# Exchanging odd v products and odd q products between two stages, and running w3's last columns in four column groups

## The chip, the cores and the metric

The kernel runs on one core of a Trainium2 chip. The core has a matrix engine (TensorE, PE in the profile, with its weight loads shown as PEld), a vector engine (VectorE, DVE), a scalar engine (ScalarE, ACT), GpSimd (POOL), and SyncE (SP), whose queue issues this kernel's DMA transfers in order. Every engine works through its own list of instructions and waits on semaphores for the others. Matmuls read SBUF and write PSUM, which has eight banks; one bank holds 128 x 512 f32 values.

The metric is the device time of one execution in microseconds (us). Lower is better.

## What is computed

A gated block over 2048 rows of 512 features, in bf16. `xn` is the layer norm of `x`; `s` is a sliding dilated attention of 32 heads of 16 features, each position looking at 8 positions, 2 apart; `g` is a token-shifting MLP.

```python
def _A_ref(x, wqkv, wo):                      # x is xn here
    qkv = transpose((x @ wqkv).reshape(B, S, 3, 32, 16), 2, 0, 3, 1, 4)
    q, k, v = qkv
    idx = pos[:, None] - 2 * arange(8)[None, :]       # positions before 0 are masked
    logits = einsum("bhsd,bhswd->bhsw", q, k[:, :, idx]) * 16 ** -0.5
    o = einsum("bhsw,bhswd->bhsd", softmax(logits), v[:, :, idx])
    return o.transpose(...).reshape(B, S, 512) @ wo

def _B_ref(x, w1, w2, w3, w4):                # w3 is 512 x 1376, w4 is 1376 x 512
    h = gelu(layernorm(x) @ w1)
    # four quarters of h's columns, shifted by +1, -1, +2, -2 rows
    x1 = x + concatenate([g0, g1, g2, g3], -1) @ w2
    return x1 + gelu(layernorm(x1) @ w3) @ w4

xn = layernorm(x)
out = x + _A_ref(xn, wqkv, wo) * silu(_B_ref(xn, w1, w2, w3, w4))
```

## The kernel before

**Rows.** The attention looks back by steps of two, so even and odd rows never meet in it. The kernel keeps them apart: `p` = 0 for the even rows, 1 for the odd ones, 1024 rows each. A chunk `c` is 512 rows of one parity: chunks 0 and 1 are even, 2 and 3 odd. `xnT[p]` holds the normalized rows transposed, features on partitions.

**Order.** Every instruction is wrapped in `pin`, which keeps it in program order on its engine, so each engine's list is as the code is written, the SP queue's too. A wait at the head of a list holds up all that is behind it.

**PSUM.** In the first stage `pair()` gives two banks at a time out of three pairs in turn (banks 0 to 5), and `single()` banks 6 and 7. The matmuls for a pair wait until the pair three before it has been read.

**First stage, lines 501 to 622.** Rows are loaded, normalized and transposed. Then, chunk by chunk, come the products: `q_all(c)` is two pairs of eight matmuls, each pair copied to `qT` by ScalarE; `k_all(c, parts, both)` the same for k, where each pair is copied twice under two head masks (with `both=False` VectorE takes half of the copies); `v_pair(p, t)` is two 128-row tiles of v, one ScalarE copy into one of two staging buffers `vst`, and two stores to `v_d` in DRAM, 256 KB each; `w1(c, a)` is half of a chunk's first MLP layer with a gelu. `w1` reads `xn2T`, which `scaled(c)` makes on VectorE from `xnT` and row factors that go through DRAM (`rows2_write`, `rows2_read`). `w2(c)` adds the second layer to the rows and takes the statistics of the second norm; `columns(c)` applies that norm and issues four transposing DMAs into `x1nT`. `v_pad` stores zero rows around v. Then `w3(c)` for four chunks: 1376 columns are ten blocks of 128 and one of 96, each block four matmuls; gelus go to `h3a` and `h3b`. In this kernel the even rows' v is computed here and the odd rows' v is not; q and k are computed here for all rows. `w4_sb` is loaded at line 599, in the middle of this stage, after `k_all(2)`.

**Attention, lines 911 to 983.** There are 18 turns `n` (`NU`), 9 for each parity. A turn issues `scores(n)` (32 small matmuls in four row groups and an exp on ScalarE into `prob`; all scores share banks 0 to 3), the minimum with a mask for the turn before (`band`), and `values(n-2)`: 32 matmuls in four column groups for the output (L675), 16 more in four column groups for the softmax denominators (L685), and a copy to `oT`. Between them TensorE is given w4's products: `g_w4(t)` is a `Group` of 11 matmuls for a tile of 128 rows, and `w4_take(k)` issues up to `k` of them in order; `q` in line 914 is a turn's quota, taken in thirds. The last product of a group lets VectorE add the bank to the rows (L800), and then a tanh and a gate follow. With each turn comes one smaller group (`small_g`): in turns 0 to 7 `g_v(n)`, one tile of the odd rows' v (four matmuls, a ScalarE copy, and a store at the turn's end); later `g_fin`, the output product with wo, for even rows. While `w4_take` runs with `extra`, the small group is issued right when a w4 group ends, and if at most 5 of the turn's quota are then left, these are dropped and made up by the next turns. Groups use banks 6 and 7 in turn through the list `free`.

Denominators of a batch of turns end in turns 5, 9, 13 and 16 (`ends`), where `inverse` makes their reciprocals on VectorE (L697) and `write_rec` stores them; `read_rec` and `apply` use them one to three turns later.

**Tail, from line 985.** The last w4 products, and the output products of the odd rows with their stores.

**Buffers.** `b8` tiles (8 KB a partition) share 11 buffers and `b4` tiles (4 KB) 10; a tile's buffer is free again after its last use. `wqk_sb` is a `b8` tile with the weights of q and k.

Of the kernel before, what the change touches and what calls it, by code (L numbers as in the profile page):

```python
# [8 lines left out]
AF = mybir.ActivationFunctionType  # L9
# [11 lines left out]
def kernel(  # L21
# [19 lines left out]
    def pin(ins):  # L41

        return tc.keep_in_program_order(ins)
# [30 lines left out]
    big = ctx.enter_context(tc.tile_pool(name="big", bufs=11))  # L74
    kbp = ctx.enter_context(tc.tile_pool(name="kbp", bufs=2))
    wpl = ctx.enter_context(tc.tile_pool(name="wpl", bufs=2))
    sm4 = ctx.enter_context(tc.tile_pool(name="sm4", bufs=10))
    fin = ctx.enter_context(tc.tile_pool(name="fin", bufs=8))
    dram = ctx.enter_context(tc.tile_pool(name="dram", bufs=1, space=bass.MemoryType.DRAM))
    psp = ctx.enter_context(tc.tile_pool(name="psp", bufs=1, space=bass.MemoryType.PSUM))  # L80
# [1 line left out]
    def b8(shape, name):  # L82
        return big.tile(shape, BF16, name=name, tag="b8")

    def b4(shape, name):
        return sm4.tile(shape, BF16, name=name, tag="b4")
# [4 lines left out]
    def pair():  # L91
        cnt["d"] += 1
        b = 2 * ((cnt["d"] - 1) % 3)
        return PS[:, b : b + 2, :]
# [11 lines left out]
            out=xn[p][:, i : i + n, :], in_=xv[p, i * P : (i + n) * P, :].rearrange("(i q) d -> q i d", q=P)  # L106
        ))

    wqk_sb = b8([P, ND, 2 * D], "wqk_sb")
    wv_sb = b4([P, ND, D], "wv_sb")  # L110
    load_x(0, 0, 1)
    load_x(0, 1, 1)
# [2 lines left out]
    load_x(0, 3, 1)  # L115
    for h in range(2):
        pin(SP.dma_start(
            out=wqk_sb[:, :, h * D // 2 : (h + 1) * D // 2], in_=wqkv_v[:, :, h * D // 2 : (h + 1) * D // 2]
        ))
    pin(SP.dma_start(out=wqk_sb[:, :, D : 2 * D], in_=wqkv_v[:, :, D : 2 * D]))  # L120
    load_x(1, 0, 2)
    load_x(1, 2, 2)
    w1_sb = b4([P, ND, D], "w1_sb")
# [166 lines left out]
    def scaled(c):  # L290
        p, k = c // 2, c % 2
        t = xn2Ts[c]
        pin(DVE.tensor_tensor(  # L293
            out=t, in0=xnT[p][:, :, k * CH : (k + 1) * CH],
            in1=t[:, ND - 1, :].unsqueeze(1).to_broadcast([P, ND, CH]), op=ALU.mult,
        ))
# [27 lines left out]
    def q_half(pts, lo, hi, nts=range(ND)):  # L324
        for nt in nts:
            for dt in range(ND):
                pin(PE.matmul(  # L327
                    pts[nt // 2][:, nt % 2, lo:hi], lhsT=wqk_sb[:, dt, nt * P : (nt + 1) * P],
                    rhs=xnT[0][:, dt, lo:hi], start=(dt == 0), stop=(dt == ND - 1),
                ))  # L330

    def proj(c, a, w, rhs):
        pt = pair()
        for b in range(2):
            nt = 2 * a + b
            for dt in range(ND):
                pin(PE.matmul(  # L337
                    pt[:, b, :], lhsT=w[:, dt, nt * P : (nt + 1) * P], rhs=rhs[:, dt, :],
                    start=(dt == 0), stop=(dt == ND - 1),
                ))  # L340
        return pt

    def chunk(t, c):
        p, k = c // 2, c % 2
        return t[p][:, :, k * CH : (k + 1) * CH]

    def q_keep(c, a, pt):
        pin(ACT.activation(chunk(qT, c)[:, 2 * a : 2 * a + 2, :], pt, AF.Copy))

    def q_all(c):  # L350
        for a in range(2):
            q_keep(c, a, proj(c, a, wqk_sb[:, :, 0:D], chunk(xnT, c)))

    def k_pad(p):
        pin(POOL.memset(kM[p][:, :, 0:8, :], 0.0))
# [2 lines left out]
    def k_all(c, parts=(0, 1), both=True):  # L358

        p, k = c // 2, c % 2  # L360
        for a in parts:
            pt = proj(c, a, wqk_sb[:, :, D : 2 * D], chunk(xnT, c))
            for e in range(2):
                dst = kM[p][:, 2 * a : 2 * a + 2, 8 + k * CH : 8 + (k + 1) * CH, e]
                sc = em[:, e : e + 1]
                if both:
                    pin(ACT.activation(dst, pt, AF.Copy, scale=sc))  # L367
                else:
                    pin(ACT.activation(dst[:, 0], pt[:, 0], AF.Copy, scale=sc))
                    pin(DVE.tensor_scalar(out=dst[:, 1], in0=pt[:, 1], scalar1=sc, scalar2=None, op0=ALU.mult))  # L370
# [40 lines left out]
    def w1(c, a):  # L411
        p, k = c // 2, c % 2
        pt = proj(c, a, w1_sb, xn2Ts[c])
        pin(ACT.activation(  # L414
            hT[p][:, 2 * a : 2 * a + 2, 1 + k * CH : 1 + (k + 1) * CH], pt, AF.Gelu_apprx_tanh
        ))
# [51 lines left out]
    def h3_of(c, ft):  # L468
        return h3a[c][:, ft, :] if ft < NA else h3b[c][:, ft - NA, :]

    def w3(c):
        x1nT = x1nTs.pop(c)
        h3a[c] = b8([P, NA, CH], "h3a")
        h3b[c] = b4([P, NF - NA, CH], "h3b")
        for a in range((NF + 1) // 2):
            pt = pair()
            fts = [ft for ft in (2 * a, 2 * a + 1) if ft < NF]
            for ft in fts:
                fs = P if ft < NF - 1 else FL
                for dt in range(ND):  # L480
                    pin(PE.matmul(  # L481
                        pt[:fs, ft % 2, :], lhsT=w3_sb[:, dt, ft * P : ft * P + fs], rhs=x1nT[:, dt, :],
                        start=(dt == 0), stop=(dt == ND - 1),
                    ))
            if len(fts) == 2:
                t, o = (h3a[c], 2 * a) if 2 * a < NA else (h3b[c], 2 * a - NA)
                pin(ACT.activation(t[:, o : o + 2, :], pt, AF.Gelu_apprx_tanh))  # L487
            else:
                pin(ACT.activation(h3b[c][:FL, NF - 1 - NA, :], pt[:FL, 0, :], AF.Gelu_apprx_tanh))

    xo = {}

# [99 lines left out]
    w1(1, 0)  # L592
    w1(1, 1)
    scaled(2)
    q_all(2)
    k_all(2, (0,))
    scaled(3)
    k_all(2, (1,), both=False)
    pin(SP.dma_start(
        out=w4_sb[:, 0 : NF - 1, :],  # L600
        in_=B_w4[0 : (NF - 1) * P, :].rearrange("(ft q) n -> q ft n", q=P),
    ))
    pin(SP.dma_start(out=w4_sb[0:FL, NF - 1, :], in_=B_w4[(NF - 1) * P : F, :]))
    w1(2, 0)
    w1(2, 1)
    w1(3, 0)
    w2(0)
    w1(3, 1)
    columns(0)
    v_pad(1)  # L610
    q_all(3)
    k_all(3)
    w2(1)
    w2(2, "a0 a1 c- s0 s1")
    w3(0)
# [4 lines left out]
        load_xo(0, i)  # L620
    for c in range(1, NCH):
        w3(c)


    pin(ACT.preload_act_table_set("exp_and_others"))
# [126 lines left out]
            out=ov[p, i * P : (i + n) * P, :].rearrange("(i q) d -> q i d", q=P), in_=xo[p][:, i : i + n, :]  # L752
        ))

    tanhs, gates, vstores = [], [], []

    free = [6, 7]

# [54 lines left out]

        return Group(NF, one, done)

    def g_v(t):
        def one(pt, dt):
            pin(PE.matmul(  # L818
                pt, lhsT=xnT[1][:, dt, t * P : (t + 1) * P], rhs=wv_sb[:, dt, :],
                start=(dt == 0), stop=(dt == ND - 1),  # L820
            ))

        return Group(ND, one, lambda pt: v_keep(1, t, 1, pt, vstores))

    stores = []
    now = {"n": 0}
# [40 lines left out]

    finals = []
    w4s = [g_w4(t, 2 if t == 15 else int(t > 12)) for t in range(16)]
    small_g = {n: [g_v(n)] for n in range(8)}  # L870
    fin0 = [g_fin(0, i, SP if i % 2 else None, later=finals) for i in range(8)]
    fin1 = [g_fin(1, 0, later=finals)]
    for n, i in zip((8, 9, 10, 12, 13, 14, 15, 16), range(8)):
# [3 lines left out]
    def flush(q):  # L877
        while q:
            q.pop(0)()
# [31 lines left out]
    load_va(0)  # L911
    for n in range(NU):
        now["n"] = n
        q = W4 * (n + 1) // NU - kept_back.get(n, 0) - unit["given"]
        extra = small_g.get(n, [])

        early = n < 8
        if n == 0:
            unit["left"] = HEAD
            w4_take(HEAD)  # L920
            unit["given"] = 0
        unit["left"] = q

        for j in range(2):
            if n == NU - 1:
                read_rec(3, 2 * j, 2)
            elif n - 1 - j in ends:
                read_rec(ends[n - 1 - j], 2 * j, 2)
        if n == 15:
            values(13)  # L930
        scores(n)
        if 1 <= n < 16:
            band(n - 1)
        if n >= 2 and n != 15:
            values(n - 2 if n < 16 else n - 1)
        if n + 1 < NU:
            load_va(n + 1)
        if n == 4:
            load_wo()
        if n != 16:  # L940
            flush(finals)
        if n in ends:
            recs[ends[n]] = inverse()
            write_rec(ends[n])
        if n == 17:
            free += [2, 3]
            pin(ACT.preload_act_table_set("silu_and_others"))
        w4_take(5 if n == 15 else q // 3)
        late = list(gates)
        gates.clear()  # L950
        flush(tanhs)
        if n == 15:
            values(14)
            apply(2, 0, 2)
        if n == 17:
            band(n)
        w4_take((q - 5) // 2 if n == 15 else q // 3, extra if early else [])
        if n < 15:
            flush(late)
        if 15 <= n < 17:  # L960
            band(n)
        if n == 16:
            flush(finals)
        w4_take(unit["left"], extra if early else [])
        if not early and n < NU - 1 and 0 < open_w4[0].at < 5:
            unit["left"] = 5 - open_w4[0].at
            w4_take(unit["left"])
        for j in range(2):
            if n < 15 and n - 2 - j in ends:
                apply(ends[n - 2 - j], 2 * j, 2)  # L970
        if n == 16:
            apply(2, 2, 2)
        if n >= 15:
            flush(late)
            flush(gates)
        while extra:
            extra.pop(0).all()

        flush(vstores)
        if n in xo_at:  # L980
            load_xo(*xo_at[n])
        if n in (12, 14):
            flush_stores(n - 1)
# [54 lines left out]
```

## Time and profile before

| what | us |
|---|---|
| median of 3 runs (lowest, highest) | 192.98 (192.38, 192.99) |
| the profiled execution | 192.83 |
| its span in the trace | 191.1 |
| ScalarE busy | 131.6 |
| VectorE busy | 114.8 |
| w3(1) to w3(3), L481, from 79.70 to the first w4 product | 28.5 |
| start of turn 0's scores | 109.59 |
| start of turn 17's w4 products | 178.62 |

The granted TensorE clock is full in every slice of the span. Positions in the trace are given in us from the span's start. A matmul of 512 columns is shown with 379 ns from start to end, while the next starts 0.216 us after it: matmuls overlap, so what they cost is read from the distances of their starts. A timeline line has the start, the length, the engine, the line of code, the operation, output and inputs, the shape and the number of instructions merged into it; in brackets the idle time before it and what ended it. Some records are missing from the trace, so a merged count can be one or two short.

### The profile page before, as it was taken

Reading aid. Unit: us, or ns where it says so; the run is one execution under the profiler, and the core shown is the slowest. Engines: PE = TensorE matmul, PEld = TensorE weight load, DVE = VectorE, ACT = ScalarE, POOL = GpSimd, SP = SyncE. Lnnn points to the kernel's source line nnn. Section 1 sums busy time; section 2 is a strip of 40 time slices with the busy share of each in tenths; the row PEclk is TensorE's granted clock in tenths of the full one; section 3 lists DMA queues with packets and bytes.
Section 4 is the critical chain, followed back from the end, with each engine's and each line's share of the span. In section 5 each row is a group of like instructions: output and inputs, shape, how many; then the busy total and the mean of one; then the engine's idle time right before and its main releaser. Section 6 shows DMA issues by size and latency. Waiting matters only on the chain.

```text
span 191.1 us, 5239 instructions
## 1 busy us (share of the span) xinstructions
PE 181.8 (95%) x2215; PEld 90.1 (47%) x2244; DVE 114.8 (60%) x227; ACT 131.6 (69%) x153; POOL 20.8 (11%) x60
## 2 busy tenths in 40 slices
PE   7899999999999999999999999999999999999991
PEld 2464444444444444444444444555454454455570
DVE  5877775232662996665000045655589699689894
ACT  7299858977268246165656796789678788867982
POOL 3015656000020022042000000000000000000000
PEclk9999999999999999999999999999999999999999
DMA  4999486478904124404610045348753874831245
GB/s 131 334 356 304 89 161 116 102 246 291 313 5 84 30 29 88 98 12 84 211 40 0 23 138 162 106 140 279 212 166 79 222 212 129 256 115 39 75 140 191
DMA packets 39859, 27.74 MB, mean 145 GB/s; under 512 B 18068, under 2 KB 39324, under 8 KB 39836
## 3 DMA queue, kind: packets, MB, share of 16 engines
q1 hardware_dynamic: 39836, 27.41, 51.7%
q8 instruction: 17, 0.28, 0.6%
q14 instruction: 6, 0.05, 0.1%
HBM read 17.14 MB, written 6.59 MB: 124 GB/s over the span
## 4 chain that ended last, share of the span: by engine, by line
PE 80%; ACT 9%; DMA 3%; DVE 3%; issue 2%; SPq 1%
PE PS L481 19%; PE PS L787 19%; PE PS L337 16%; PE PS L441 5%; ACT kM L367 5%; PE PS L840 4%; PE PS L675 3%; DMA wqk_sb<-in_A_wqkv_dram 3%; PE PS L818 3%; PE PS L649 3%; PE PS L376 3%; PE PS L685 2%; PE PS L327 1%; DVE sg L855 1%; DVE xo L857 1%
## 5 line engine op out<-in xcount | busy, mean ns | idle before, releaser
L481 PE MATMUL PS<-x1nT,w_sb 128*128 128x512 bf16 (+1 forms) x173 | 38.2, 379 | 0.2
L656 ACT ACTIVATE prob<-PS 128x1824 bf16<-128x1824 f32 x18 | 30.4, 1687 | 0.9 <-ACT sig L807 0.7
L487 ACT ACTIVATE h3a<-PS 128x1024 bf16<-128x1024 f32 x16 | 16.4, 1024 | 20.6 <-PE PS L481 19.4
L787 PE MATMUL PS<-w_sb,h3a 128*128 128x512 bf16 x112 | 28.8, 379 | 1.4 <-issue 1.1
L800 DVE TENSOR_TENSOR xn<-PS,xn 128x512 bf16<-128x512 f32 x15 | 10.2, 682 | 32.5 <-PE PS L787 32.3
L481 PEld LDWEIGHTS <-w_sb 128*128 128x128 bf16 (+1 forms) x176 | 17.6, 100 | 20.4
L337 PE MATMUL PS<-xnT,wqk_sb 128*128 128x512 bf16 x110 | 24.9, 379 | 0.2
L661 DVE TENSOR_TENSOR prob<-prob,maskb 128x1824 bf16<-128x1824 bf16 x18 | 19.8, 1101 | 1.3 <-ACT prob L656 1.3
L367 ACT ACTIVATE kM<-PS,em 128x1024 bf16<-128x1024 f32 x14 | 18.3, 1403 | 2.3 <-PE PS L337 2.3
L787 PEld LDWEIGHTS <-h3a 128*128 128x128 bf16 x128 | 11.4, 97 | 13.0
L337 PEld LDWEIGHTS <-wqk_sb 128*128 128x128 bf16 x112 | 10.9, 98 | 13.2 <-issue 0.4
L449 DVE TENSOR_TENSOR xn<-PS,xn 128x1024 bf16<-128x1024 f32 x8 | 9.6, 1214 | 11.3 <-PE PS L441 11.3
L840 PE MATMUL PS<-wo_sb,oT 128*128 128x512 bf16 (+1 forms) x80 | 15.5, 336 | 0.0
L387 ACT ACTIVATE vst<-PS 128x512 bf16<-128x512 f32 (+1 forms) x12 | 8.9, 738 | 8.8 <-issue 3.4
L847 ACT ACTIVATE sg<-PS 128x512 bf16<-128x512 f32 (+1 forms) x20 | 10.1, 512 | 6.8 <-PE PS L840 6.5
L441 PE MATMUL PS<-w_sb,hT 128*128 128x512 bf16 x63 | 14.4, 379 | 0.1
L337 PE MATMUL PS<-xn2T,w_sb 128*128 128x512 bf16 x62 | 14.4, 379 | 0.1
L787 PE MATMUL PS<-w_sb,h3b 128*128 128x512 bf16 (+1 forms) x44 | 12.8, 380 | 1.0 <-issue 1.0
L414 ACT ACTIVATE hT<-PS 128x1024 bf16<-128x1024 f32 x8 | 8.0, 1034 | 5.1 <-PE PS L337 4.8
L224 DVE BATCH_NORM_STATS2 l1s<-xn 128x6 f32<-128x512 bf16 x16 | 10.2, 681 | 1.9 <-DMA xn<-in_A_x_dram 1.9
L840 PEld LDWEIGHTS <-oT 128*128 128x128 bf16 x80 | 7.8, 98 | 6.3 <-issue 0.6
L293 DVE TENSOR_TENSOR xn2T<-xnT,xn2T 128x2048 bf16<-128x2048 bf16 x4 | 4.9, 1217 | 9.4 <-DMA r_d<-r2t 4.9
(106 smaller groups left out, 228.2 us busy)
## 6 DMA issues: line engine op xcount, KB each, us to landing
ring<-v_d SPq DMA_DIRECT2D x18, 256.0 KB
v_d<-vst SPq DMA_DIRECT2D x16, 256.0 KB, 3.5
xo<-in_A_x_dram SPq DMA_DIRECT2D x8, 256.0 KB, 3.5
ring<-rec_d SPq DMA_DIRECT2D x8, 228.0 KB, 3.7
out_dram<-xo SPq DMA_DIRECT2D x7, 256.0 KB, 3.4
xn<-in_A_x_dram SPq DMA_DIRECT2D x6, 256.0 KB, 5.6
w_sb<-in_B_w_dram SPq DMA_DIRECT2D x1, 1376.0 KB
w_sb<-in_B_w_dram SPq DMA_DIRECT2D x1, 1280.0 KB
```

What stands on the lines that cost most here:

```text
L224: pin(DVE.bn_stats(out=self.st[:, j, :], in_=self.src[:, j, :]))
L337: pin(PE.matmul(pt[:, b, :], lhsT=w[:, dt, nt * P : (nt + 1) * P], rhs=rhs[:, dt, :], start=(dt == 0), stop=(dt == ND - 1),))
L367: pin(ACT.activation(dst, pt, AF.Copy, scale=sc))
L441: pin(PE.matmul(pt[:, j, :], lhsT=w2_src(p, g, m0), rhs=w2_sb[:, g, :], start=(g == 0), stop=(g == ND - 1),))
L481: pin(PE.matmul(pt[:fs, ft % 2, :], lhsT=w3_sb[:, dt, ft * P : ft * P + fs], rhs=x1nT[:, dt, :], start=(dt == 0), stop=(dt == ND - 1),))
L487: pin(ACT.activation(t[:, o : o + 2, :], pt, AF.Gelu_apprx_tanh))
L656: pin(ACT.activation(pr, S_ps[:, :, 0 : ND * NQ], AF.Exp, scale=SCALE))
L661: pin(DVE.tensor_tensor(out=f, in0=f, in1=maskb[:], op=ALU.min))
L787: pin(PE.matmul(pt, lhsT=h3_of(c, ft)[:fs, jj * P : (jj + 1) * P], rhs=w4_sb[:fs, ft, :], start=(ft == 0), stop=(ft == NF - 1 and silu < 2),))
L800: pin(DVE.tensor_tensor(out=x_i, in0=pt, in1=x_i, op=ALU.add))
L840: pin(PE.matmul(pt[:, 0:W], lhsT=oT[p][:, dt, i * P : (i + 1) * P], rhs=wo["sb"][:, dt, c], start=(dt == 0), stop=(dt == ND - 1),))
L847: pin(ACT.activation(sg["t"][:, c], pt[:, 0:W], AF.Copy, scale=2.0 if half else 1.0))
```

## The change

In the first stage the odd rows' q (`q_all(2)`, `q_all(3)`) goes out and the odd rows' v (`v_pair(1, 0)`, `2`, `4`, `6`) comes in, spread between `w1`, `w2` and `k_all`; the two loads of w4 are issued later, behind the last of these v pairs. In the attention's turns 0 to 7 the small group is now `g_q`, four matmuls and a ScalarE copy, in place of `g_v`. q's and k's weights become two `b4` tiles, and `b4` has 11 buffers.

`w3` now runs the ten full blocks alone. The last 96 columns of all four chunks are computed in `w3_last`, between `w3(2)` and `w3(3)`: three rounds, in each of which the four column groups of TensorE hold 32 of the columns for different chunks. Round `i` does all 96 columns of chunk `i` in groups 0 to 2, and a third of chunk 3's in group 3.

In the attention the quota of turns 0 to 3 counts two more products, and the reciprocals of turns 9 and 13, with their stores, come after the second third of w4's products.

```diff
-    sm4 = ctx.enter_context(tc.tile_pool(name="sm4", bufs=10))
+    sm4 = ctx.enter_context(tc.tile_pool(name="sm4", bufs=11))
...
-    wqk_sb = b8([P, ND, 2 * D], "wqk_sb")
+    wq_sb = b4([P, ND, D], "wq_sb")
+    wk_sb = b4([P, ND, D], "wk_sb")
...
     def w3(c):
-        x1nT = x1nTs.pop(c)
+        x1nT = x1nTs[c]
         h3a[c] = b8([P, NA, CH], "h3a")
-        h3b[c] = b4([P, NF - NA, CH], "h3b")
-        for a in range((NF + 1) // 2):
+        h3b_of(c)
+        for a in range(NF // 2):
...
+    def w3_last():
+        last = NCH - 1
+        pts = [pair(), pair()]
+        for i in range(last):
+            pt = pts[i // 2][:, i % 2, :]
+            for dt in range(ND):
+                for j in range(NCH):
+                    c, part = (i, j) if j < last else (last, i)
+                    f = (NF - 1) * P + 32 * part
+                    pin(PE.matmul(
+                        pt[32 * j : 32 * j + 32, :], lhsT=w3_sb[:, dt, f : f + 32], rhs=x1nTs[c][:, dt, :],
+                        start=(dt == 0), stop=(dt == ND - 1), tile_position=(0, 32 * j),
+                    ))
+            pin(ACT.activation(h3b_of(i)[:FL, NF - 1 - NA, :], pt[:FL, :], AF.Gelu_apprx_tanh))
+            pin(ACT.activation(
+                h3b_of(last)[32 * i : 32 * i + 32, NF - 1 - NA, :], pt[FL:P, :], AF.Gelu_apprx_tanh
+            ))
...
     scaled(2)
-    q_all(2)
     k_all(2, (0,))
+    k_all(2, (1,), both=False)
     scaled(3)
-    k_all(2, (1,), both=False)
+    w1(2, 0)
+    w1(2, 1)
+    v_pair(1, 0)
+    w1(3, 0)
+    v_pair(1, 2)
+    w2(0)
+    w1(3, 1)
+    columns(0)
+    v_pad(1)
+    v_pair(1, 4)
+    k_all(3, (0,))
+    v_pair(1, 6)
     pin(SP.dma_start(
         out=w4_sb[:, 0 : NF - 1, :],
...
-    w1(2, 0)
-    w1(2, 1)
-    w1(3, 0)
-    w2(0)
-    w1(3, 1)
-    columns(0)
-    v_pad(1)
-    q_all(3)
-    k_all(3)
+    k_all(3, (1,))
     w2(1)
...
     for c in range(1, NCH):
         w3(c)
+        if c == 2:
+            w3_last()
...
-    def g_v(t):
+    def g_q(k, nt):
         def one(pt, dt):
             pin(PE.matmul(
-                pt, lhsT=xnT[1][:, dt, t * P : (t + 1) * P], rhs=wv_sb[:, dt, :],
+                pt, lhsT=wq_sb[:, dt, nt * P : (nt + 1) * P], rhs=xnT[1][:, dt, k * CH : (k + 1) * CH],
                 start=(dt == 0), stop=(dt == ND - 1),
             ))
-        return Group(ND, one, lambda pt: v_keep(1, t, 1, pt, vstores))
+        def done(pt):
+            pin(ACT.activation(qT[1][:, nt, k * CH : (k + 1) * CH], pt, AF.Copy))
+        return Group(ND, one, done)
...
-    small_g = {n: [g_v(n)] for n in range(8)}
+    small_g = {n: [g_q(n // ND, n % ND)] for n in range(8)}
...
-        q = W4 * (n + 1) // NU - kept_back.get(n, 0) - unit["given"]
+        q = W4 * (n + 1) // NU + 2 * (n < 4) - kept_back.get(n, 0) - unit["given"]
...
-        if n in ends:
+        if n in (5, 16):
             recs[ends[n]] = inverse()
             write_rec(ends[n])
...
         w4_take((q - 5) // 2 if n == 15 else q // 3, extra if early else [])
+        if n in (9, 13):
+            recs[ends[n]] = inverse()
+            write_rec(ends[n])
```

## The prediction

> **What bounds the kernel.** I read the page's busy times and its chain first, then TensorE's own timeline, looking for places where one matmul starts later than the one before it allows.
>
> ```profile
> PE 181.8 (95%) x2215; PEld 90.1 (47%) x2244; DVE 114.8 (60%) x227; ACT 131.6 (69%) x153; POOL 20.8 (11%) x60
> PE 80%; ACT 9%; DMA 3%; DVE 3%; issue 2%; SPq 1%
> ```
>
> TensorE is busy 95% of the span and is 80% of the chain. Back to back, 512-column matmuls start every 0.216 us (in the third fence below, 32 of L441 take 59.62 to 66.53, which is 32 x 0.216). So between 10 and 180 us an edit counts only by what it does to the sum of TensorE's starts, or to one of its few small pauses. The pauses are found by adding counts of 0.216 us to a start and comparing with the next start. Four bear on this change.
>
> The first two are in the first stage and at its end:
>
> ```profile
> 58.09 5.16 ACT L367 ACTIVATE kM<-PS,em 128x1024 bf16<-128x1024 f32 x4 [0.70 <-PE PS L337]
> 110.35 1.69 ACT L656 ACTIVATE prob<-PS 128x1824 bf16<-128x1824 f32 x1
> ```
> ```profile
> 59.62 7.30 PE L441 MATMUL PS<-w_sb,hT 128*128 128x512 bf16 x32
> ...
> 111.01 1.03 PE L818 MATMUL PS<-wv_sb,xnT 128*128 128x512 bf16 x4
> 112.09 0.41 PE L649 MATMUL PS<-qT,kM 32*128 32x57 bf16 x32
> ```
>
> The 32 of L441 are w2(1) and w2(2). They end by count at 66.53, and the next matmul of L481 starts at 66.75: 0.22 us lost. The four k copies on ScalarE (58.09 to 63.25) hold the bank that w2(2) wants at 63.07. In the attention, the v group from 111.01 is issued by 111.87, scores come 0.10 us behind a full matmul elsewhere (115.67 to 115.77), so 111.97; they start at 112.09, when exp(0) has ended (110.35 + 1.69 = 112.04): 0.12 us lost.
>
> The other two are in turns 9 and 13. Turn 9:
>
> ```profile
> 144.01 1.67 PE L787 MATMUL PS<-w_sb,h3a 128*128 128x512 bf16 x7
> 144.20 0.86 DVE L697 RECIPROCAL rec<-PS 128x114 bf16<-128x114 f32 x1
> 144.98 0.62 DVE L800 TENSOR_TENSOR xn<-PS,xn 128x512 bf16<-128x512 f32 x1
> 145.66 1.02 PE L840 MATMUL PS<-wo_sb,oT 128*128 128x512 bf16 x4
> ```
>
> Seven w4 products end by count at 145.52. L840 starts at 145.66, right after VectorE's addition (144.98 to 145.60), which frees its bank, and that addition stood behind the reciprocal. 0.14 us lost; in turn 13 the same (159.61 by count, 159.78 in fact) loses 0.17.
>
> **w3's last columns, the one cut in TensorE's sum.** Removed: 16 matmuls of 96 columns, which take a full start each: 16 x 0.216 = 3.45 us. Added: 48 of 32 columns, 12 steps of four column groups. No row has 512 moving columns in this form; the nearest are the denominators and the values.
>
> ```profile
> L481 PE MATMUL PS<-x1nT,w_sb 128*96 128x512 bf16 x16 | 4.1, 379 | 0.0
> L675 PE MATMUL PS<-prob,ring 128*32 128x57 bf16 x576 | 7.7, 193 | 0.0
> L685 PE MATMUL PS<-prob,den_st 128*32 128x114 bf16 x256 | 6.1, 214 | 0.0
> ```
> ```profile
> 116.45:116.50 0.05, 0.05 (x24) 1.00 0.00 0
> 116.50:116.55 0.05, 0.05 (x20) 1.00 0.00 0
> 116.55:116.60 0.05, 0.05 (x16) 1.00 0.00 0
> 116.60:116.65 0.05, 0.05 (x12) 1.00 0.00 0
> ```
>
> The last fence counts TensorE's matmuls in flight in windows of 50 ns while one turn's denominators end: four finish in each, so four column groups, each with moving data of its own, share the time of one. By the chain 16 of them take 0.21 us: 52.5 ns a step of 114 columns. 114 columns at the pace of 512 in 0.213 are 47.5 ns, so a step has 5 ns on top. For 512 columns that gives 0.218 (12 steps: 2.62 us); if the whole 52.5 grew with the columns, 0.236 (2.83); by the values, whose 32 start 0.25 us ahead of the next form (31 ns a step of 57 columns), 0.281 (3.37). I take 2.70, near the row with more columns. Changing form costs 0.10 us from full to tiled (above) and 0.12 back: the denominators start at 116.35, 0.20 of them end at 116.55, the next full matmul starts at 116.67. Gain 3.45 - 2.70 - 0.22 = **0.53 us**; ends: 0.61 gained to 0.14 lost. ScalarE swaps four gelus of 583 ns for three of them and three of 32 partitions. None has run; bounds are the 383 ns of a 128x256 copy and the 597 of a 128x512 one, so at most 1.3 us more, under w3(3)'s matmuls, where ScalarE waits about 0.7 us before each gelu. Without that cover the first bank would come back late for w3(3)'s second pair; it is due there 1.7 us after the tiled part and is read by then.
>
> **q and v change places.** 32 matmuls of 0.216 us leave each stage and 32 enter it: 0. ScalarE pays 1019 ns for a v pair and 1024 for a q pair; in the attention a v copy has 597, as the same shape has in L847. 0. By count w2(0) and w2(1) start where they did (47.53, 59.62). What changes is the order of ScalarE's copies: a v copy now stands between the two k parts of chunk 3. k part 0 is copied from 56.37 to 59.0, v to 60.0, part 1 to 62.7, ahead of the 63.07 at which its bank is wanted (both pairs before them are wanted at 59.62 and 61.35, later than 59.0 and 60.0). The first pause goes: **0.22 us**. What is late next is w1(2,0): q_all(2) no longer stands ahead of it, so it is wanted at 38.90 and not 42.35, and its operand, scaled(2), ends at 37.16 + 1.23 = 38.39. The slack falls from 4 us to 0.5. I cost it at 0; a read of r2 that lands 1 us later would cost 0.5.
>
> **The queues.** Eight stores of v (565 ns each on SP, 3.5 us to landing) leave turns 0 to 7 and go to 45 to 66 us, where SP idles from 46.3 to 56.9. The first v copy (ScalarE, 44.3) needs the buffer whose stores were issued at 38.47 and 39.1 and land by 43.2 at the longest landing, 4.1. The load of w4 moves behind columns(0)'s transposes, v_pad (which ended at 63.0) and four stores (2.6 us): issued near 65.6 instead of 43.05. Its two issues took 0.5 and 2.66 us, so SP is free by 68.8, before columns(1)'s transposes come at 69.69. Its 1.38 MB at the 315 to 410 GB/s of 46 to 52 us take some 4 us, to 70. columns(1)'s last transpose is issued by 74.8 and lands 2.4 later, at 77.2; w3(1) wants it at 79.5. Cost 0, under 2.3 us of cover. w4's first product comes at 107.
>
> **Attention.** The first turn now gives 11 w4 products in place of 5. Its quota rises from 9 to 11, and after the running group's five, with the small group behind it, 6 are left, one more than the rule drops. TensorE wants scores(1) 4.98 + 0.10 us after w3's end. ScalarE ends w3 with a pair (0.20 later, 1.02), then the table load 1.28 and exp 1.70: 4.22. The second pause goes: **0.12**. With the old quota TensorE would want it at 3.88 and wait 0.34. In turn 1 five products and four of q take 1.94 us; scores(2) want exp(1) 2.23 us after scores(1) and come at 2.38. By turn 5 the count is the old one (45). New loss: the next w4 group takes a bank that VectorE is still adding from, 0.94 us after the last product, with 0.86 of q between: **-0.08**. Moving the reciprocals of turns 9 and 13 behind the addition frees that bank by 144.9: **0.14 + 0.17**. Behind them on VectorE stand a gate and the minimum for the next turn, which start no later overall; the store of rec goes 0.6 us later, and its read is applied two turns on.
>
> **Sum:** 0.53 + 0.22 + 0.12 - 0.08 + 0.31 = 1.10 us. The profiled execution took 192.83 (span 191.1, the rest around it): 191.73. The median of the three runs is 0.15 above it: 191.88. I say **191.8**.
>
> **Rivals.**
> *Tiled steps at the slow end.* At 0.281 us a step the cut becomes a loss of 0.14 and 0.43 us are left: 192.4 to 192.55. For it: the longest tiled run seen lasts 0.3 us. Against: more columns brought the time per column down, from 0.55 to 0.46 ns.
>
> *Weight loads come out from under the matmuls (slower).* Each of the 48 has a load of its own, and the denominators' loads last 95 ns. If a column group could not load while it streams, the four loads of a step would show in a row: 12 x 4 x 0.095 = 4.6 us, so 191.73 + 4.6 = 196.3; if the four ran together, 1.1 us, about no change. It decides from 0.09 us a step. Against: 16 denominators would then take 4 x (47.5 + 95) = 570 ns, and they take 210.
> The Trainium skill, page "TensorE: Matmul & The Clock Gate", Part 3, "The mechanism", states this very rule: a weight load overlaps running matmuls only when its row group differs, and here all four have the same rows. The trace's 210 ns disagrees with it.
>
> *w4's load holds up columns(1) (slower).* At the span's mean of 124 GB/s its 1.38 MB would take 11 us, to 77, and the transposes behind it would land up to 5 us late; 2.3 are covered: 194.4. Against: the same load ran at over 300 GB/s next to w3's.
>
> *The change does not do what it says:* the kept pauses return elsewhere (w1(2,0), the vst buffers), and with the cut 192.2 to 192.8 results.
>
> **Chances.** Forecast 0.68 (its own range 191.3 to 192.2), slow tiled steps 0.14, weight loads 0.06, w4's load 0.06, pauses elsewhere 0.06. 0.3% (0.58 us, about what a measurement of this kernel can tell from no change) puts the bounds at 192.40 and 193.56. Forecast, with a third of the two mixed cases: faster 0.74. The rest of these and the mild form of the weight loads: same 0.16. Slower 0.10. The range goes down to 191.2, where a step would cost the bare 0.213 and a further small pause go, and up to 192.8 for the mixed cases.
>
> **What would show it.** The tiled part should last about 2.9 us from w3(2)'s last full matmul to w3(3)'s first; steps over 0.3 us prove the loads rival. w3(0) should start 0.2 us earlier, with no gap at w1(2,0). L840 in turns 9 and 13 should follow at once. A wait of L481 for a DMA of x1nT would prove the rival of w4's load. I am wrong if TensorE has new gaps in the order from k_all(2) on, or if the tail after the last w4 product lengthens.

## The result, and the profile after

After the change six executions took 191.11 to 191.48 us, median 191.2; six of the kernel before had the median 192.97. The ratio is 0.9908 (95% interval 0.9885 to 0.993): 1.8 us faster. 191.8 was forecast, with 191.3 to 192.2 as the forecast's own range; 191.2 lies below it, at the very edge of the wider range, and the gain is 1.6 times the 1.1 us of the sum. The profiled execution took 191.11, with a span of 189.4 (before: 191.1).

The page of the kernel after, busy times and chain:

```profile
PE 183.9 (97%) x2276; PEld 89.2 (47%) x2276; DVE 114.8 (61%) x227; ACT 132.8 (70%) x155; POOL 20.4 (11%) x60
PE 86%; DVE 5%; ACT 4%; DMA 2%; SPq 1%; issue 0%
```

TensorE sets the end even more than before. Its busy time went up although its work went down: this trace misses no matmul records, the one before missed 29. Starts are the measure. "issue", time in which an engine waited for nothing that the profile shows, had 2% of the chain and now has 0%.

TensorE's timeline after, from w2(1) to the first w4 products (start, length, engine, line, operation, tiles, shape, count):

```profile
59.62 7.07 PE L442 MATMUL PS<-w_sb,hT 128*128 128x512 bf16 x32
66.52 8.80 PE L486 MATMUL PS<-x1nT,w_sb 128*128 128x512 bf16 x40
...
78.61 17.43 PE L486 MATMUL PS<-x1nT,w_sb 128*128 128x512 bf16 x80
95.97 2.77 PE L504 MATMUL PS<-x1nT,w_sb 128*32 128x512 bf16 x48
98.68 8.81 PE L486 MATMUL PS<-x1nT,w_sb 128*128 128x512 bf16 x40
107.32 1.46 PE L814 MATMUL PS<-w_sb,h3a 128*128 128x512 bf16 x6
```

w2(1) starts at 59.62 in both kernels: the exchange of v and q moved nothing. w3(0) starts at 66.52 (before 66.75), straight behind the 32 matmuls. The tiled part lasts 2.71 us to the next full matmul. The 80 matmuls of w3(1) and w3(2) end by count at 95.88, 0.09 us ahead of it.

Turn 9's products and the output product behind them, and turn 15's scores:

```profile
143.10 1.68 PE L814 MATMUL PS<-w_sb,h3a 128*128 128x512 bf16 x7
144.61 1.03 PE L870 MATMUL PS<-wo_sb,oT 128*128 128x512 bf16 x4
...
163.94 0.40 PE L676 MATMUL PS<-qT,kM 32*128 32x57 bf16 x32
164.27 0.60 PE L814 MATMUL PS<-w_sb,h3a 128*128 128x512 bf16 x2
```

Seven products from 143.10 end by count at 144.61, and L870 starts then: no pause. Turn 15's scores run through. Before, they did not. This is TensorE's timeline of the kernel before in turns 15 and 16:

```profile
165.11 0.34 PE L649 MATMUL PS<-qT,kM 32*128 32x57 bf16 x21
165.67 0.26 PE L649 MATMUL PS<-qT,kM 32*128 32x57 bf16 x11 [0.23 <-issue]
...
170.42 0.54 PE L675 MATMUL PS<-prob,ring 128*32 128x57 bf16 x32
```

Of 32 scores 21 were issued; the next started 0.41 us after the 21st, where these scores otherwise follow each other every 10 ns. The 32 values of turn 16 take 0.54 where every other turn has 0.42. No wait for another engine is shown at either place. Where the 1.7 us of the span come from, by the starts of the same instruction in the two traces:

| from that start on | before | after | gained up to there | by this stage |
|---|---|---|---|---|
| w3(0) | 66.75 | 66.52 | 0.23 | 0.23 |
| first w4 product | 108.19 | 107.32 | 0.87 | 0.64 |
| turn 5's scores | 127.64 | 126.72 | 0.92 | 0.05 |
| turn 10's scores | 146.62 | 145.57 | 1.05 | 0.13 |
| turn 14's scores | 160.74 | 159.56 | 1.18 | 0.13 |
| turn 16's scores | 170.09 | 168.50 | 1.59 | 0.41 |
| the identity product in the tail (L792, L819) | 180.13 | 178.43 | 1.70 | 0.11 |
| end of the span | 191.1 | 189.4 | 1.7 | 0 |

The last 0.52 us, in turns 15 and 16, have no term in the sum. They are what the experiments were for.

### The profile page after: what moved, and what is told of

Read it like the earlier page. It is cut to its first block, busy times and chain, and to the rows that moved or that the text cites. A ratio compares the mean times of both kernels' runs of the same rounds, so it can differ in the third digit from the quotient of the medians.

```text
span 189.4 us, 5337 instructions
## 1 busy us (share of the span) xinstructions
PE 183.9 (97%) x2276; PEld 89.2 (47%) x2276; DVE 114.8 (61%) x227; ACT 132.8 (70%) x155; POOL 20.4 (11%) x60
## 4 chain that ended last, share of the span: by engine, by line
PE 86%; DVE 5%; ACT 4%; DMA 2%; SPq 1%; issue 0%
PE PS L814 21%; PE PS L486 18%; PE PS L338 14%; PE PS L442 7%; PE PS L377 6%; PE PS L870 4%; PE PS L845 4%; PE PS L702 3%; PE PS L676 3%; ACT kM L368 3%; DMA xn<-in_A_x_dram 2%; PE PS L712 2%; DVE sg L885 1%; DVE xo L887 1%; PE PS L504 1%; PE PS L328 1%
## 5 line engine op out<-in xcount | busy, mean ns | idle before, releaser
L486 PE MATMUL PS<-x1nT,w_sb 128*128 128x512 bf16 x160 | 35.0, 379 | 0.0
L814 PE MATMUL PS<-w_sb,h3a 128*128 128x512 bf16 x128 | 32.1, 380 | 0.0
L486 PEld LDWEIGHTS <-w_sb 128*128 128x128 bf16 x160 | 15.5, 98 | 19.1 <-issue 0.4
L870 PE MATMUL PS<-wo_sb,oT 128*128 128x512 bf16 (+1 forms) x80 | 15.5, 336 | 0.0
L377 PE MATMUL PS<-wv_sb,xnT 128*128 128x512 bf16 x64 | 15.0, 379 | 0.0
L338 PE MATMUL PS<-xnT,wk_sb 128*128 128x512 bf16 x64 | 14.8, 379 | 0.1
L814 PE MATMUL PS<-w_sb,h3b 128*128 128x512 bf16 (+1 forms) x48 | 13.4, 380 | 0.0
L388 ACT ACTIVATE vst<-PS 128x1024 bf16<-128x1024 f32 x8 | 8.2, 1019 | 4.4 <-PE PS L377 2.9
L870 PEld LDWEIGHTS <-oT 128*128 128x128 bf16 x80 | 7.8, 98 | 6.0
L225 DVE BATCH_NORM_STATS2 l3s<-xn 128x6 f32<-128x512 bf16 x16 | 10.3, 683 | 0.2
```

Source lines behind the costliest of these rows:

```text
L225: pin(DVE.bn_stats(out=self.st[:, j, :], in_=self.src[:, j, :]))
L338: pin(PE.matmul(pt[:, b, :], lhsT=w[:, dt, nt * P : (nt + 1) * P], rhs=rhs[:, dt, :], start=(dt == 0), stop=(dt == ND - 1),))
L377: pin(PE.matmul(pt, lhsT=xnT[p][:, dt, t * P : (t + 1) * P], rhs=wv_sb[:, dt, :], start=(dt == 0), stop=(dt == ND - 1),))
L486: pin(PE.matmul(pt[:, b, :], lhsT=w3_sb[:, dt, ft * P : (ft + 1) * P], rhs=x1nT[:, dt, :], start=(dt == 0), stop=(dt == ND - 1),))
L814: pin(PE.matmul(pt, lhsT=h3_of(c, ft)[:fs, jj * P : (jj + 1) * P], rhs=w4_sb[:fs, ft, :], start=(ft == 0), stop=(ft == NF - 1 and silu < 2),))
L870: pin(PE.matmul(pt[:, 0:W], lhsT=oT[p][:, dt, i * P : (i + 1) * P], rhs=wo["sb"][:, dt, c], start=(dt == 0), stop=(dt == ND - 1),))
```

## Experiments

Each median stands beside that of the kernel before in the same batch (192.87, 193.05 and 192.94), whose own executions scatter by 1.5 us and more; so a few tenths are read from the traces, and the medians must agree. A trace is one execution.

### Are the two pauses at a fixed place?

**The kernel before, once more.**

> The kernel before once more, unchanged, for a second trace. In its first trace TensorE stopped in the middle of turn 15's scores (after 21 of 32 matmuls, 0.34 us) and in the middle of turn 16's values (0.12 us), 254 instructions later, and no wait of any engine is shown there; after the change both are gone. Theory A (place): TensorE's instructions arrive in blocks of some 256, a block came late while the DMA engines were full, and the change only moved all instructions of the attention by 64 places; then the two pauses stand again at the same two instructions, and the time is 192.9 to 193.0. Rival B (traffic): the pauses come from the transfers of that moment, which the exchange of v and q changed; then they stand near these turns, but not at the same instruction. Rival C (chance): they come and go; then one or both are missing here and the time is nearer to 192.4.

192.94, ratio 0.9992 (0.9963 to 1.0021). Its timeline at turn 15:

```profile
164.90 0.34 PE L649 MATMUL PS<-qT,kM 32*128 32x57 bf16 x21
166.01 0.26 PE L649 MATMUL PS<-qT,kM 32*128 32x57 bf16 x11 [0.78 <-issue]
```

Again after the 21st score, and longer. The second pause was not there. So in turn 15 the place is fixed and the length is not: theory A with a part of C.

**Only the place shifted.**

```diff
-    for i in range(10):
+    for i in range(42):
         pin(PE.matmul(
-            PS[:, 6 + i % 2, :], lhsT=ones_bf[:], rhs=ones_bf.unsqueeze(1).to_broadcast([P, TPC, P]),
+            PS[:, 6 + i % 2, 0:122], lhsT=ones_bf[:], rhs=ones_bf[:, 0:122],
```

> The kernel before, with the 10 warm-up matmuls of 512 columns at its start cut into 42 of 122 columns: the same number of columns, 32 matmuls and 32 weight loads more, nothing else. Nothing is saved in the sum. Theory A (place): the two pauses of turns 15 and 16 go, 192.4 to 192.5. Rivals B and C: 192.9 to 193.0 with the pauses where they were or nearby.

192.47 against 192.87, ratio 0.9973 (0.9949 to 0.9998). Turn 15's 32 scores run through in its trace, and turn 16's values too:

```profile
165.01 0.40 PE L649 MATMUL PS<-qT,kM 32*128 32x57 bf16 x32
```

Nothing behind the warm-up changed, so the place matters.

**The tiled part alone, and the change without it.**

```diff
-    sm4 = ctx.enter_context(tc.tile_pool(name="sm4", bufs=10))
+    sm4 = ctx.enter_context(tc.tile_pool(name="sm4", bufs=11))
...
     for c in range(1, NCH):
         w3(c)
+        if c == 2:
+            w3_last()
```

> The kernel before with w3's last columns in four column groups alone. Its trace after the change shows 107.32 - 98.68 and 98.68 - 95.97: the tiled part lasts 2.71 us, and w3(1) to w3(3) with it are 0.64 us shorter than before. Expected from that: 0.64 us less, 192.3. It also puts 32 matmuls and 32 weight loads ahead of the attention. Theory A (place) adds the loss of the two pauses of turns 15 and 16 (0.4 and 0.1 us): 191.75 to 191.9. Rival B (traffic) keeps them: 192.3. In the prediction's terms the tiled part alone was 0.53: 192.4.

192.33 against 192.87, ratio 0.9973 (0.9952 to 0.9994). TensorE's timeline:

```profile
96.09 2.77 PE L503 MATMUL PS<-x1nT,w_sb 128*32 128x512 bf16 x48
...
111.72 0.41 PE L672 MATMUL PS<-qT,kM 32*128 32x57 bf16 x32 [0.43 <-ACT prob L679]
```

The tiled part has its 2.77 us, and no pause is left in turns 15 and 16, as A has it. The median shows less than A's price, which left out the second row: w3 now ends with a whole pair's gelu ahead of the table load, the quota is the old one, and scores(1) wait 0.43 us for exp(0), where the kernel before lost 0.12.

```diff
     for c in range(1, NCH):
         w3(c)
-        if c == 2:
-            w3_last()
```

> The kernel after the change with w3 as it was before (16 matmuls of 96 columns), all else changed. It loses the 0.64 us of the tiled part: 191.85. Theory A (place): its attention stands at the old 64 places earlier, so the two pauses come back: 192.3 to 192.4. Rival B (traffic): they stay away, 191.8 to 191.9.

191.87 against 192.87, ratio 0.9967 (0.9939 to 0.9994). Here A missed: the attention stands at the same place as before, and the pauses stay away. So the old place alone does not bring them back: something else in the change keeps them away too.

### What else is needed?

**The exchange alone** (the change without tiled part, quota and reciprocals).

> The exchange of v and q, the later load of w4 and the split of q's and k's weights alone; w3, quota and reciprocals as before. The prediction's step: the pause of 0.22 us ahead of w3(0) goes, all else 0, so 0.2 us less. Rival B (the exchange removes the pauses of turns 15 and 16): 0.75 less.

192.71 against 193.05, ratio 0.9986 (0.9966 to 1.0007). At turn 15:

```profile
164.98 0.34 PE L653 MATMUL PS<-qT,kM 32*128 32x57 bf16 x22
166.01 0.26 PE L653 MATMUL PS<-qT,kM 32*128 32x57 bf16 x10 [0.69 <-issue]
```

The pause stands: rival B, in which the exchange removes it, falls. The forecast's own step is there: w2(1) starts at 59.42 and w3(0) at 66.33, which is 32 x 0.216 and no pause. A new stop of 0.2 us stands in turn 8's denominators, as in the next run.

**The reciprocals alone.**

```diff
-        if n in ends:
+        if n in (5, 16):
             recs[ends[n]] = inverse()
             write_rec(ends[n])
...
         w4_take((q - 5) // 2 if n == 15 else q // 3, extra if early else [])
+        if n in (9, 13):
+            recs[ends[n]] = inverse()
+            write_rec(ends[n])
```

> The kernel before with nothing but the reciprocals of turns 9 and 13 behind the second third of w4's products. The prediction's step: 0.14 + 0.17 = 0.31 us less, with L840 following at once in both turns. Theory A in the form that is left after the first four runs (the pauses need both the place, TensorE's instruction 3749 in turn 15, and a block of instructions whose transfer starts late): the place stays, TensorE and the transfers of turns 13 to 15 shift by some tenths, so both outcomes are open; with the pauses 0.3 us less than before, without them 0.8 less. If the exchange of v and q were what removes them (rival B), they stay: 0.3 less.

192.28 against 193.05, ratio 0.9967 (0.9947 to 0.9987): 0.77 us. At turns 9, 8 and 15:

```profile
144.12 1.67 PE L787 MATMUL PS<-w_sb,h3a 128*128 128x512 bf16 x7
145.63 0.59 PE L840 MATMUL PS<-wo_sb,oT 128*128 128x512 bf16 x2
```
```profile
139.33 0.60 PE L685 MATMUL PS<-prob,den_st 128*32 128x114 bf16 x16
...
164.93 0.40 PE L649 MATMUL PS<-qT,kM 32*128 32x57 bf16 x32
```

L840 follows seven products at once (144.12 + 1.51), and the pause of turn 15 is gone as well, at an unchanged place. In this trace turn 8's denominators take 0.60 where 0.39 is usual: a stop of 0.2 us that the kernel before did not have. On SP the stores of the reciprocals and the xo load behind them went from 159.21 and 160.56 to 159.79 and 161.13.

**One load moved.**

```diff
-    xo_at = {9: (1, 0), 11: (1, 6), 12: (1, 2), 13: (1, 4)}
+    xo_at = {9: (1, 0), 11: (1, 6), 12: (1, 2), 16: (1, 4)}
```

> The kernel before with one transfer moved: the 256 KB load of xo for rows that are needed only in the tail is issued at the end of turn 16 in place of turn 13 (160.56 us, just ahead of the late block). If traffic of data is what makes the block late, both pauses go: 0.5 us less. If the block's start hangs on TensorE's own progress alone, they stay: no change.

192.49 against 193.05, ratio 0.9974 (0.9957 to 0.999). SP, and turn 15's scores:

```profile
159.35 1.30 SPq L706 DMA_DIRECT2D rec_d<-rec  x2
162.24 0.57 SPq L709 DMA_DIRECT2D ring<-rec_d  x1
```
```profile
165.25 0.40 PE L649 MATMUL PS<-qT,kM 32*128 32x57 bf16 x32
```

With nothing issued between 160.65 and 162.24 the scores run through. So the transfers ahead of the pause matter, as the place does.

**What is late.** The profile's DMA view has a queue of the kind "instruction" (q8), with one packet of 16 KB at a time: 17 in the kernel before, where TensorE has 2244 weight loads and as many matmuls, 4488 instructions (17 x 256 are 4352). Two answers for windows of 0.1 us, the kernel before at 163.2 and its repeat at 163.7:

```profile
q8 instruction: 1, 0.02, 58.4%
```
```profile
q8 instruction: 1, 0.02, 59.2%
```

Such a packet begins there. The percentage is the share of 16 DMA engines in 0.1 us, so the first packet took 58.4% of 1.6 us, 0.93 us. Set against the end of the pause that follows, for the stops inside runs of small matmuls that cost 0.1 us or more, with one exception in turn 14 of "old reciprocals" (below):

| kernel | TensorE's instruction at which it stopped | packet begins | it takes | TensorE goes on | after the packet's begin | after its end |
|---|---|---|---|---|---|---|
| before, turn 15 | 3749 | 163.24 | 0.93 | 165.67 | 2.43 | 1.50 |
| before, turn 16 | 4003 | 168.26 | 0.96 | 170.69 | 2.43 | 1.47 |
| before again, turn 15 | 3749 | 163.76 | 0.95 | 166.01 | 2.25 | 1.30 |
| exchange alone, turn 8 | 2475 | 136.85 | 1.11 | 139.43 | 2.58 | 1.47 |
| exchange alone, turn 15 | 3751 | 163.54 | 0.96 | 166.01 | 2.47 | 1.51 |
| reciprocals alone, turn 8 | 2473 | 136.58 | 1.73 | 139.70 | 3.12 | 1.39 |
| tiled part twice (below), turn 6 | 2221 | 130.41 | 1.03 | 132.75 | 2.34 | 1.31 |
| tiled part twice, turn 13 | 3495 | 157.07 | 0.95 | 159.49 | 2.42 | 1.47 |
| k and q in turns (below), turn 5 | 1967 | 124.77 | 0.92 | 127.17 | 2.40 | 1.48 |

The stops lie on one grid of 254 to 255 listed instructions, within two (1967, 2221, 2475, then 4 x 255 to 3495, 3749, 4003), in five different programs, and TensorE goes on 1.30 to 1.51 us after a packet has ended. Where turn 15 shows no pause, the packet had ended earlier: with the reciprocals alone it ran from 161.69 to 163.06, with the load moved from 162.39 to 163.63, which is 2.0 and 1.75 us before instruction 3749 started (165.05 and 165.38). With only the place shifted the packet began at 160.51, 4.2 us before instruction 3749 (there a weight load of the denominators) was due; in the two traces of the kernel before it began 2.0 and 1.3 us before that. If the grid is carried through all fourteen traces and the n-th packet is set against its n-th place (the 7th is 1967), none of 232 blocks is begun less than 1.30 us after its packet's end. So the pauses are waits for the next block of TensorE's instructions. The Trainium skill, page "Runtime: NRT & Kernel Launch", section "Instruction fetch mechanics", states blocks of 16 KiB, 256 instructions, which an engine fetches ahead over a DMA queue of its own; the grid and the packets agree. It also states that this is hidden because instructions are dispatched more slowly than they are fetched; here gaps of 0.13 to 0.96 us from one start to the next show, among small matmuls that are issued 8 to 13 ns apart. Why a packet begins late was tried only through the xo load and the reciprocals; which data it stands behind is open.

### The terms of the sum, one by one

**Old quota in the first turns.**

```diff
-        q = W4 * (n + 1) // NU + 2 * (n < 4) - kept_back.get(n, 0) - unit["given"]
+        q = W4 * (n + 1) // NU - kept_back.get(n, 0) - unit["given"]
```

> The kernel after the change with the old quota in turns 0 to 3 (5 products of w4 in the first turn, not 11). The prediction's step: scores(1) are wanted 3.88 us after w3's end and exp(0) ends at 4.22, so TensorE waits 0.34 us there for ScalarE, and the 0.08 us at the bank that VectorE still adds from go: 0.25 us more than after, 191.3. Rival: the later turns give the wait back, because what is wanted there is late too; then 191.05.

191.70 against 192.94, ratio 0.9933 (0.9909 to 0.9957); the change itself had 191.05 and 0.9907 in an earlier batch. The wait is there, in the timeline of this kernel:

```profile
111.66 0.41 PE L676 MATMUL PS<-qT,kM 32*128 32x57 bf16 x32 [0.43 <-ACT prob L683]
```

From turn 0's scores to turn 5's it needs 18.44 us, the change 18.00. The step had 0.25; 0.44 it is, and no later turn gives it back. exp(0) ends 4.22 us after w3's end, as forecast, but scores(1) are wanted 3.77 us after it and not 3.88, and start 0.05 us behind the exp.

**Old reciprocals.**

```diff
-        if n in (5, 16):
+        if n in ends:
...
-        if n in (9, 13):
-            recs[ends[n]] = inverse()
-            write_rec(ends[n])
```

> The kernel after the change with the reciprocals of turns 9 and 13 where they were. The prediction's step: L840 waits 0.14 us in turn 9 and 0.17 us in turn 13: 0.3 us more than after, 191.35. All instructions stand 64 places later than before, so by the place half of theory A the pauses of turns 15 and 16 stay away although the loads of data in turn 13 are again where they were; if the reciprocals alone had removed them, they come back: 191.9.

191.48 against 192.94, ratio 0.9931 (0.9906 to 0.9956); 0.43 more than 191.05. Turns 9 and 14:

```profile
143.02 1.68 PE L814 MATMUL PS<-w_sb,h3a 128*128 128x512 bf16 x7
144.67 1.02 PE L870 MATMUL PS<-wo_sb,oT 128*128 128x512 bf16 x4
...
160.10 0.55 PE L702 MATMUL PS<-prob,ring 128*32 128x57 bf16 x32
```

L870 is due at 144.53 and starts at 144.67: 0.14, as forecast. Turn 13 (155.76 to 159.77 between scores, 3.81 in the change) loses 0.20. Turn 15's scores run through. A small pause of 0.13 appears in turn 14's values. It stands at instruction 3615, off the grid above, and its cause is open. The intervals of this run and the one before it overlap that of the change, so the steps rest on the traces.

**The tiled part twice.**

```diff
-            for dt in range(ND):
+            for dt in [*range(ND), *range(ND)]:
                 for j in range(NCH):
```

> The kernel after the change with each round of the tiled part computed twice (the second pass starts its sums afresh, so the output is the same): 48 matmuls, 12 steps more, with no change of form in between. The disputed cost by itself. At 0.218 us a step (the streaming of 512 columns and 5 ns on top) 2.62 us more; at the denominators' time per column 2.83; at the values' 3.37; if weight loads came out from under the matmuls, 3.7 or more.

194.3, ratio 1.0067 (1.0044 to 1.0091), 3.25 more than the change. The timeline:

```profile
95.76 5.36 PE L504 MATMUL PS<-x1nT,w_sb 128*32 128x512 bf16 x96
...
158.79 0.30 PE L702 MATMUL PS<-prob,ring 128*32 128x57 bf16 x16
159.49 0.30 PE L702 MATMUL PS<-prob,ring 128*32 128x57 bf16 x16 [0.40 <-issue]
```

96 last 5.36, 48 last 2.77: 12 steps more cost 2.59, 0.216 a step. That is a full matmul's pace, with nothing on top and no weight load showing. The other 0.66 us go with new pauses of the kind above, now that 96 more instructions stand ahead of the attention: turn 13, shown here, loses 0.58 in this trace, and turn 6 0.37.

**A version that should be faster still.**

```diff
-    q_all(1)
-    k_all(1)
+    for a in range(2):
+        k_all(1, (a,))
+        q_keep(1, a, proj(1, a, wq_sb, chunk(xnT, 1)))
```

> The kernel after the change with chunk 1's k and q pairs taking turns (k, q, k, q in place of q, q, k, k). One pause of the first stage is left in it: the matmul after w1(1,1) is due at 35.22 and starts at 35.45, when the four k copies end. With a q copy between them the first pair of k is read by 29.4 and the last by 33, ahead of the 33.5 at which its bank is wanted: 0.23 us less than after, 190.8. Rival: the pause moves to w1(1,0) or w1(1,1): no change.

190.97, ratio to before 0.9893 (0.9868 to 0.9919); the change in its own repeat 191.05, 0.9907 (0.9879 to 0.9934). The pause it aims at is gone, and another has come, in TensorE's weight loads of turn 5:

```profile
31.56 3.62 PE L338 MATMUL PS<-xn2T,w_sb 128*128 128x512 bf16 x16
35.01 3.62 PE L338 MATMUL PS<-xnT,wk_sb 128*128 128x512 bf16 x16
```
```profile
126.84 0.13 PEld L713 LDWEIGHTS <-den_st 128*32 128x32 bf16 x5
...
127.17 0.17 PEld L713 LDWEIGHTS <-den_st 128*32 128x32 bf16 x11 [0.20 <-issue]
```

31.56 and 16 x 0.216 is 35.01. Turn 5 takes 2.99 us from scores to scores where the change takes 2.73: the 0.23 are given back to a late block. It can't be told from the change.

**The change once more.**

> The kernel after the change once more. 191.2, no pause inside the scores or values of any turn, and little spread; if the pauses of turns 15 and 16 were chance (rival C), one of them shows up here and the time is up to 191.7.

191.05 (190.88 to 191.38), ratio 0.9907 (0.9879 to 0.9934), no pause inside scores or values. In all twelve executions the change scatters by 0.6 us, the kernel before by more than 1.5.

## Why the prediction was right and wrong

**Right:** that TensorE's starts set the time, and that a pause ahead of w3(0) (0.22; measured 0.23), one in turn 9 (0.14; 0.13) and one in turn 13 (0.17; 0.18) would go, by the mechanisms named. In the table of stages turn 13 shows as 0.13, because turn 11 lost 0.05. The exchange cost nothing at w2(0) and w2(1), and the last k copy ended at 62.49 (62.7 forecast), ahead of 63.07. w4's load was issued at 65.92 (65.6) and no L486 waited for x1nT; scaled(2) ended at 37.75, more than 1 us ahead of its use. Turn 0 gained 0.05 (0.12 - 0.08 in the sum): the bank that VectorE still reads lost 0.08 (111.00 by count, 111.08 in the trace).

**Mis-sized:** the cut itself, by a little. "I take 2.70, near the row with more columns", with 0.10 and 0.12 for the change of form, gave 0.53; the runs showed 12 x 0.216 = 2.59 and 0.09 + 0.12, so 0.65 by count, 0.64 between starts. The 5 ns on top of a step, taken from steps of 114 columns, do not show at 512. They were worked out with 0.213 us for 512 columns, which no run shows: 80 matmuls of L486 in 17.43 us have 0.216 from start to start. Perhaps the runs of denominators are too short to tell a pace from their edges; that was not tried. The rival of the weight loads is out: twelve steps more cost 2.59, not 3.7.

**Missing:** "Four bear on this change" was the step that failed. The trace of before has six pauses that the change touches. The split of turn 15's scores in 21 and 11, marked "issue", and turn 16's 0.54 were in the same timeline and had no term: 0.41 and 0.11 of the 1.7 us. The prediction gives no reason for leaving them out. They are waits for a block of TensorE's own instructions, and the change reaches them in two ways, each shown enough by itself in one trace and a median of 12 executions: 64 more instructions ahead of the attention (the shift), and later stores and loads in turn 13 (the reciprocals). The wider range went down to 191.2 for the case that "a further small pause" goes, so the kind was foreseen there, but not which pause, nor why, nor that two would go. Up to turn 14 the stages gained 1.18 us (0.23 + 0.64 + 0.05 + 0.13 + 0.13), close to the 1.10 of the sum.

## What to carry to other kernels

Where one engine's starts are the time, list every one of its pauses before the edit is priced, those marked "issue" too, and ask of each whether the edit moves the instruction count or the transfers ahead of it. An edit that only changes how many instructions stand ahead of a dense run of small matmuls can cost or gain some tenths of a microsecond: the shift by 64 gained 0.4, and with the 96 of the doubled part 0.66 went beyond the work itself. Blocks of under 128 output columns with 512 moving ones can be worth packing into column groups: here 48 quarter matmuls took the time of 12, and the change of form and back cost 0.21 us.

## What was not expected of the hardware

- Four column groups with four different moving operands of 512 columns run at a full matmul's pace, 0.216 us a step, with 48 weight loads hidden.
- TensorE stands still for 0.13 to 0.96 us, from one start to the next, for a block of its own instructions when the block's packet comes late; it goes on 1.30 to 1.51 us after the packet has ended.
- A gelu of 32 partitions by 512 takes 0.59 us on ScalarE, the same as one of 96.
